# The last chunk's second product as seven half-size products, with its outputs finished one after another, and the second half starting with the chunk at the change

## The chip, the cores and the metric

The kernel runs on one core of one Trainium2 chip. The metric is the device time of one execution in microseconds (us). Engines are called as the profile calls them: PE is TensorE (matmul), PEld its weight load, DVE is VectorE, ACT is ScalarE, POOL is GpSimd, SP is SyncE, whose queue issues all DMAs here.

## The reference

```python
xn = layernorm(x)                                  # x: 2048 tokens x 576, fp32
q, k, v = phi(xn @ wq), phi(xn @ wk), xn @ wv      # 32 heads of 18
s = (phi(q) (phi(k)^T v) / (phi(q) sum phi(k))) @ wo
g = silu(gelu(xn @ w1 + b1) @ w2 + b2)             # 576 -> 4608 -> 576
out = x + s * g
```

The change lies in the last line but one and in the last: the end of the feed-forward part `g`, and the gate `x + s * g`.

## The kernel before

Each fp32 operand is split into a rounded part and a rest ("hi" and "lo"), and each product is hi·hi + hi·lo + lo·hi: a product of two operands is three matmuls. ACT makes the hi part (`set_hi`, a cast), then DVE the lo part (`set_lo`, a subtraction of two SBUF operands).

After the attention part (to about 279 us) comes the feed-forward part. The 2048 tokens are taken in two halves of 1024, and the 4608 hidden columns in `NC = 9` chunks of four blocks of 128, so there are 18 chunk steps; `step` counts them, and `base = 28 * step` is the place of a step in the plan. One step is:

- two "up" products (`Up`, pairs `n = 2 * step` and `2 * step + 1`), each a 2x2 block product done by seven half-size products (Strassen-Winograd) in the order `UP`; each of the seven is 7 matmuls of 512 columns. Between them DVE adds partial sums in PSUM and ACT applies the gelu: this gives eight tiles `g` of 128x512 (two token halves b, two column parities, two pairs `pr`);
- a "down" product with w2, again seven half-size products (`product`, `ORDER`). Product i has left operand `h[i, pr]` (made from the `g` tiles: sums `HOps.S` on POOL for i = 7, 5, 6, 3, then a cast on ACT, then a split on DVE) and right operand `W2.ops[i]`. Each product is done in two parts, `q2 = 0` and `q2 = 2`, for two of four blocks of 128 tokens each: 12 matmuls of 288 columns into one PSUM tile, which DVE then adds into `macc` in SBUF (line 1357).

DVE, ACT, POOL and PE run their instructions strictly in the order in which the code issues them (`in_order`); functions are issued at numbered places (`add(base + at, ...)`, `at_step`), and the tables `PH`, `X_AT`, `W2_NEXT` give these numbers. The SP queue is ordered by a scheduler.

In the first half of the steps the operands of w1 and w2 are made from the raw weights and stored to DRAM (`keep_op`); the second half loads them back, chunk 0 first (`n % NP`, `n % NC`).

The last step (`plain`) does not use the seven products for its down product. It loads the raw w2 of chunk 8, splits it (in step 16) and runs a plain product (`down_plain`, line 1467): eight blocks of 128 tokens one after another, 24 matmuls each. For each block DVE adds the sum to `macc` (line 1462), ACT applies the silu (line 1463), DVE multiplies by s (1420) and adds x (1421; for block 6 POOL does), and a DMA writes the rows (1422). The last block is split into 384 and 192 columns. The eight `h` operands (names `hp`) are casts and splits of `g` without sums. Before it POOL adds the shared term U1 to three parts of `macc` (`combine`, line 1367).

Of the kernel before, what the change touches and what calls it, by code (L numbers as in the profile page):

```python
# [15 lines left out]
P = 128  # L16
# [22 lines left out]
NWARM = 20  # L39

# [4 lines left out]
def linear_attention_gated_ffn(ctx, tc, x, xT, wqkv, wo, w1, w1e, b1, w2, b2, out):  # L45
# [78 lines left out]
    w1_dram, w2_dram = {}, {}  # L124

# [512 lines left out]
    def load_w2_raw(n):  # L638
        raw = w2rp.tile([P, 4, CF // 2, HD], F32, tag="w2raw", name=f"w2raw{n}")
        nc.sync.dma_start(raw.rearrange("p b a d -> p (b a d)"), w2[n % NC])  # L640
        return raw
# [207 lines left out]
    def load_we(n):  # L849

        we_sb[n] = w1p.tile([P, WB, P], F32R, tag="we", name=f"we_{n}", bufs=2)
        dst = we_sb[n].bitcast(F32).rearrange("p b c -> p (b c)")
        g, q = divmod(n % NP, WG)
# [8 lines left out]
    class W1:  # L862


        def __init__(self, n):
            self.n = n
            raw = stage_w1(f"w1raw{n}")
            nc.sync.dma_start(raw, w1[n % NP])
# [43 lines left out]
    class W1Loaded(W1):  # L912


        def __init__(self, n):
            self.n, self.tiles = n, {}
            for i in ("a", "c", "d"):
                if i == "c":
                    t = w1r.tile([P, 8, P], F32R, tag="stw", name=f"wc_{n}")
                else:  # L920
                    t = w1_tile(i, n)
                self.tiles[i] = t
                nc.sync.dma_start(t.bitcast(F32), w1_dram[n % NP, i])

    def load_six(n):

        t = w1_tile("e", n)
        for k in range(2):
            six[n + k] = t[:, 4 * k : 4 * k + 4]
            nc.sync.dma_start(six[n + k].bitcast(F32), w1_dram[(n + k) % NP, 6])  # L930
# [240 lines left out]
    class Up:  # L1171
        late = []

        def __init__(self, n, w, xs):
            self.p, self.w = n % NP, w
# [36 lines left out]
        def step(self, i):  # L1212
# [12 lines left out]
            elif i == 6:  # L1225
                self.mm(A, 6, first=False)
                nc.scalar.copy(u1_sb, A)  # L1227
                if self.p:
                    self.gelu(0, 0, B)
            elif i == 5:  # L1230
                self.mm(E, 5)
                nc.scalar.copy(m5_sb, E)
                if not self.p:
                    self.gelu(0, 0, B)
# [15 lines left out]
    class W2:  # L1250
# [21 lines left out]
        def plain(self, f):  # L1272
            k = 2 - 2 * (f % 2)
            self.src["p", f] = self.raw[:, k : k + 2, f // 2]

        def hi(self, i):
            tag = ORDER[i[1]] if isinstance(i, tuple) else i
            self.tiles[i], self.ops[i] = op_tile(fr, [2, HD], f"w2_{tag}", 1, f"w2_{self.n}_")
# [7 lines left out]
        def load(self, i):  # L1286
            t, self.ops[i] = op_tile(fr, [2, HD], f"w2_{i}", 1, f"w2_{self.n}_")
            nc.sync.dma_start(t.bitcast(F32), w2_dram[self.n % NC, i])

    class HOps:  # L1290
# [28 lines left out]
        def hi(self, i, pr):  # L1319
            self.ops[i, pr] = hi_lo(gp, [P, 512], f"h{HBUF[i, pr]}", 1, f"h{i}{pr}_")  # L1320
# [12 lines left out]
    }  # L1333
    ORDER = (1, 2, 7, 4, 5, 3, 6)
    CHAIN = {2: 1, 3: 5, 4: 7}
# [36 lines left out]
    tails = {}  # L1372

    def load_xs(t):
        F = lambda v: v.bitcast(F32)
        flat = lambda v: F(v).rearrange("p a b -> p (a b)")[:, :D]
        if t == 0:
            xt, s_t = flat(w1_tile("a", "x0")), stage_w1("s0")[:, :D]
        elif t == 1:
            xt = flat(w1_tile("a", "x1"))  # L1380
            s_t = flat(w1p.tile([P, WB, P], F32R, tag="we", name="s1", bufs=2))
        elif t == 2:
            xt, s_t = (flat(w1_tile("a", f"{v}2")) for v in "xs")
        elif t == 3:
            xt, s_t = stage_w1("x3")[:, :D], flat(w1_tile("a", "s3"))
        elif t == 4:
            raw = F(fr.tile([P, 2, D], F32R, tag="w2_5", name="xs4", bufs=1))
            xt, s_t = raw[:, 0], raw[:, 1]
        else:
            if t == 5:  # L1390
                tails["h"] = F(x_hi(2, "xs56")).rearrange("p a b -> p (a b)")
                tails["l"] = F(x_lo(2, "xs7")).rearrange("p a b -> p (a b)")
            v = {5: tails["h"], 6: tails["h"][:, 2 * D :], 7: tails["l"]}[t]
            xt, s_t = v[:, :D], v[:, D : 2 * D]
        nc.sync.dma_start(xt, x[t * P : (t + 1) * P, :])
        nc.sync.dma_start(s_t, s_dram[t])
        tails["xs", t] = xt, s_t

    def tail_split(b, f):
        src = h.A[f // 2, b, f % 2]  # L1400
        if b == 0:
            pair = hi_lo(gp, [P, 512], f"h{f}", 1, f"hp{f}_")
        else:
            k = f % 2
            if f < 2 and ("t", 0) not in tails:
                tails["t", 0] = x_lo(0, "hp0")
            if f >= 2 and ("t", 1) not in tails:
                tails["t", 1] = x_lo(1, "hp1")
            t = tails["t", f // 2]
            pair = t[:, 2 * k, :], t[:, 2 * k + 1, :]  # L1410
        set_hi(pair, src)
        tails["hs", b, f] = pair, src

    def tail_lo(b, f):
        pair, src = tails["hs", b, f]
        set_lo(pair, src, nc.vector)

    def gate(t, c, xt, s_t, cs=slice(0, D), eng=nc.vector):

        nc.vector.tensor_tensor(s_t[:, cs], c[:, cs], s_t[:, cs], op=MUL)  # L1420
        eng.tensor_tensor(s_t[:, cs], s_t[:, cs], xt[:, cs], op=ADD)
        nc.sync.dma_start(out[t * P : (t + 1) * P, cs], s_t[:, cs])


# [26 lines left out]
    def down_plain(t, ws):  # L1451

        bi, q = divmod(t, QH)
        cs = slice(q * P, (q + 1) * P)
        seq = []
        for f, (wh, wl) in enumerate(ws):
            hh, hl = tails["hs", bi, f][0]
            seq += [(hh, wh), (hh, wl), (hl, wh)]
        dst = c_tile(bi, q).rearrange("p n d -> p (n d)")

        def end(ps, c):
            nc.vector.tensor_tensor(c, ps, c, op=ADD)
            nc.scalar.activation(c, c, AF.Silu)

        def mm(ps, w, i):
            st, w_all = seq[i]
            nc.tensor.matmul(  # L1467
                ps, st[:, cs], w_all.rearrange("p n d -> p (n d)")[:, w],
                start=(i == 0), stop=(i == len(seq) - 1),
            )  # L1470

        if t < 7:
            ps = bank2(f"pd{t}")
            for i in range(len(seq)):
                for h in range(2):
                    mm(ps[:, h, :HD], slice(h * HD, (h + 1) * HD), i)
            end(ps[:, :, :HD], as2(dst))
            gate(t, dst, *tails["xs", t], eng=nc.gpsimd if t == 6 else nc.vector)
            return

        parts = [slice(0, 384), slice(384, D)]
        ps = []
        for k, w in enumerate(parts):
            n = w.stop - w.start
            ps.append(bank1(f"pd{t}_{k}")[:, :n])
            for i in range(len(seq)):
                mm(ps[k], w, i)
        for k, w in enumerate(parts):
            end(ps[k], dst[:, w])
        for w in parts:  # L1490
            gate(t, dst, *tails["xs", t], cs=w)
# [60 lines left out]
    )  # L1552
    plans = {}
# [20 lines left out]
    for step in range(n_chunks):  # L1574
# [3 lines left out]
        h = HOps(c)  # L1578
# [21 lines left out]
        elif not plain:  # L1600
# [3 lines left out]
            if step + 2 < n_chunks:  # L1604
                make(W2, w2t, step + 1)
                for i, at in W2_NEXT.items():
                    add(base + at + 10 * change, lambda i=i, n=step + 1: w2t[n].load(i))
            else:
                make(W2, w2t, step + 1)

                w = w2t[step + 1]
                add(base + 7, w.load_raw)
                for f in range(CF):
                    add(base + 22 + f, lambda f=f, w=w: (w.plain(f), w.hi(("p", f))))
                    add(base + 24 + f, w.lo, ("p", f))
        if not plain:
# [8 lines left out]
            for what in ("S", "hi", "lo"):  # L1625
                for (i, pr), at in PH[what].items():
                    add(base + at, getattr(h, what), i, pr)
# [14 lines left out]
        if plain:  # L1642
            for m in (C12, C21, C22):
                add(base + 4, combine, m, nc.gpsimd)
            for t, at in enumerate((6, 7, 12, 13, 5, 12, 12, 12)):
                add(base + at, load_xs, t)
            for b, f, at, lo in (
                (0, 0, 7, 8), (0, 1, 8, 9), (1, 0, 10, 10), (1, 1, 10, 11), (0, 2, 11, 12),
                (0, 3, 12, 13), (1, 3, 13, 13), (1, 2, 13, 13),
            ):  # L1650
                add(base + at, tail_split, b, f)
                add(base + lo, tail_lo, b, f)
# [7 lines left out]
        if plain:  # L1660
            break
# [7 lines left out]
    ws = [w2t[step].ops["p", f] for f in range(CF)]  # L1669
    for t in range(2 * QH):  # L1670
        down_plain(t, ws)
# [47 lines left out]
```

## Time and profile before

| what | value |
|---|---|
| median of 3 runs | 1092.71 us (1092.48 to 1092.85) |
| profiled execution, its own time | 1092.45 us |
| span of its trace | 1090.6 us |
| busy: PE, DVE, ACT, POOL | 1082.6, 798.2, 549.2, 454.6 us |
| one down product of a step (168 matmuls) | 22.39 us |
| last down product (192 matmuls) | 25.71 us, from 1060.17 us |
| last matmul to end of span | 4.7 us |

The profiled execution's time lies 1.85 us above its span. In the rows of the trace the first number is the start in us from the span's beginning, the second the duration; "xN" merges N instructions; the bracket gives the idle time of the engine ahead of it and what ended that.

### The profile page before, as it was taken

The page shows a single profiled execution, that of the slowest core. Times are in us where ns is not written, and L with a number is a line of the kernel's source. Part 1 is how long each engine was busy: PE and PEld are TensorE (multiplying, and loading weights), DVE is VectorE, ACT ScalarE, POOL GpSimd, SP SyncE. Part 2 cuts the span into 40 slices and gives each one's busy share as a digit, 9 for nine tenths or more (in the row PEclk, how much of TensorE's full clock was granted, in tenths as well). Part 3 has the DMA queues.
Part 4 walks back from the last instruction along what each step waited for, and adds up shares of the span by engine and source line. Part 5 has one row for each costly group of instructions (what it writes and reads, how often), then busy time and mean ns, then how long its engine had stood idle before and what let it go on. Part 6 is the DMA issues. An engine that isn't in the chain of part 4 may idle for free.

```text
span 1090.6 us, 18119 instructions
## 1 busy us (share of the span) xinstructions
PE 1082.6 (99%) x6704; PEld 1007.4 (92%) x6704; DVE 798.2 (73%) x1099; ACT 549.2 (50%) x956; POOL 454.6 (42%) x391
## 2 busy tenths in 40 slices
PE   9999999999999999999999999999999999999998
PEld 8999999999898998988989989899898998988988
DVE  7776559888688898888988988657475574664856
ACT  6545476455646456465564654624335244252552
POOL 3555414332547455464555553414325143341340
PEclk9999999999999999999999999999999999999999
DMA  7999635675958659576595669968676666767452
GB/s 239 239 222 214 212 105 192 213 246 183 343 222 316 219 192 334 170 294 237 204 330 181 258 235 408 379 233 308 224 232 214 211 228 223 231 219 222 132 184 87
DMA packets 87266, 254.58 MB, mean 233 GB/s; under 512 B 11783, under 2 KB 24071, under 8 KB 84490
## 3 DMA queue, kind: packets, MB, share of 16 engines
q1 hardware_dynamic: 87178, 253.42, 69.7%
q8 instruction: 53, 0.87, 0.3%
q14 instruction: 35, 0.29, 0.1%
HBM read 156.57 MB, written 94.58 MB: 230 GB/s over the span
## 4 chain that ended last, share of the span: by engine, by line
PE 98%; DVE 1%; SPq 0%; ACT 0%; DMA 0%; issue 0%; POOL 0%; POOLq 0%
PE pm L1351 35%; PE a L1189 16%; PE bc L1189 10%; PE e L1189 10%; PE pk L317 6%; PE ps_s L813 5%; PE pq L317 5%; PE pv L317 4%; PE pd L1467 2%; PE ps_kva L378 1%; PE ptp L795 1%; PE warm L365 0%; PE ps_kw L728 0%; PE ps_kvb L378 0%; DMA wa_rest0q<-xh 0%; SPq L963 0%
## 5 line engine op out<-in xcount | busy, mean ns | idle before, releaser
L1357 DVE TENSOR_TENSOR macc<-pm,macc 128x576 f32<-128x576 f32 x218 | 164.4, 754 | 55.5 <-PE pm L1351 54.9
L837 ACT CAST h_h<-g 128x512 fp32r<-128x512 f32 x204 | 122.6, 620 | 132.2 <-PE pm L1351 131.6
L840 DVE TENSOR_TENSOR h_l<-g,h_h 128x512 fp32r<-128x512 f32 x204 | 154.6, 769 | 14.9 <-ACT h_h L837 13.9
L1317 POOL TENSOR_TENSOR mid<-g 128x512 f32<-128x512 f32 x34 | 44.0, 1293 | 134.9 <-ACT g L1205 134.9
L1218 ACT COPY mid<-a 128x512 f32<-128x512 f32 x36 | 21.1, 587 | 110.3 <-PE a L1189 110.1
L1224 DVE TENSOR_TENSOR bc<-bc,mid 128x512 f32<-128x512 f32 x36 | 25.1, 698 | 51.5 <-PE bc L1189 40.7
L1311 POOL TENSOR_TENSOR g<-g 128x512 f32<-128x512 f32 x34 | 52.2, 1535 | 20.8 <-ACT h_h L837 16.7
L883 POOL TENSOR_TENSOR w1raw<-w1raw 128x256 f32<-128x256 f32 x18 | 13.3, 737 | 113.9 <-ACT h_h L837 65.3
L1237 DVE TENSOR_TENSOR z<-a,mid 128x512 f32<-128x512 f32 x36 | 25.1, 698 | 46.6 <-PE a L1189 46.6
L1439 POOL TENSOR_TENSOR fin1l<-fin1h,fin1l 128x288 f32<-128x288 f32 x8 | 6.5, 808 | 122.8 <-DMA fin1l<-s_dram 57.9
L1314 POOL TENSOR_TENSOR g<-g 128x512 f32<-128x512 f32 x34 | 52.6, 1546 | 7.6 <-DVE h_l L840 5.5
L1308 POOL TENSOR_TENSOR g<-g 128x512 f32<-128x512 f32 x34 | 50.3, 1481 | 2.7
L778 POOL TENSOR_TENSOR pbuf<-phiq,den 128x576 f32<-128x576 f32 x16 | 19.0, 1188 | 61.2 <-DVE den L777 57.8
L1227 ACT COPY mid<-a 128x512 f32<-128x512 f32 x36 | 21.2, 588 | 44.3 <-PE a L1189 44.3
L1238 ACT COPY mid<-a 128x512 f32<-128x512 f32 x36 | 21.1, 587 | 40.0 <-DVE z L1237 40.0
L840 DVE TENSOR_TENSOR h_l<-mid,h_h 128x512 fp32r<-128x512 f32 x34 | 38.0, 1118 | 2.4 <-ACT h_h L837 2.4
L317 PE MATMUL pk<-wkv_h,xh 128*128 128x288 f32 (+1 forms) x160 | 38.2, 321 | 0.5 <-DVE xh L245 0.5
L317 PE MATMUL pk<-wkv_l,xh 128*128 128x288 f32 (+1 forms) x160 | 38.3, 322 | 0.1
L317 PE MATMUL pq<-wq_h,xh 128*128 128x288 f32 x160 | 34.7, 298 | 0.7 <-DVE phiq L336 0.7
L813 PE MATMUL ps_s<-kw_h,th 128*128 128x288 f32 x160 | 35.2, 302 | 0.0
L765 POOL TENSOR_TENSOR eq<-phiq,zb 128x576 f32<-128x576 f32 x16 | 22.9, 1432 | 27.6 <-DMA zb<-z_dram 19.4
L317 PE MATMUL pq<-wq_l,xh 128*128 128x288 f32 x160 | 34.3, 296 | 0.0
(891 smaller groups left out, 3709.0 us busy)
## 6 DMA issues: line engine op xcount, KB each, us to landing
we<-we_dram SPq DMA_DIRECT2D x36, 448.0 KB, 5.7
w2raw<-w SPq DMA_DIRECT2D x10, 1152.0 KB
w1raw<-w SPq DMA_DIRECT2D x18, 512.0 KB, 4.8
op_a<-wa SPq DMA_DIRECT2D x18, 512.0 KB, 4.6
op_c<-wc SPq DMA_DIRECT2D x18, 512.0 KB, 4.2
op_d<-wd SPq DMA_DIRECT2D x18, 512.0 KB, 2.7
wc<-op_c SPq DMA_DIRECT2D x18, 512.0 KB, 4.6
wa<-op_a SPq DMA_DIRECT2D x18, 512.0 KB, 5.0
```

The source lines that it names most:

```text
L317: nc.tensor.matmul(ps[:, h, : ws.stop - ws.start], st, w[:, k, ws], start=(begin and i == 0), stop=(end and i == len(seq) - 1), skip_group ...
L813: nc.tensor.matmul(ps[:, h, :HD], st[:, k, :], w[:, k, h * HD : (h + 1) * HD], start=(i == 0), stop=(i == len(seq) - 1),)
L837: nc.scalar.copy(pair[0], src)
L840: eng.tensor_tensor(pair[1], src, pair[0].bitcast(F32), op=SUB)
L1189: nc.tensor.matmul(ps, st, mv, start=first and n == 0, stop=n == len(seq) - 1, skip_group_check=True,)
L1224: tt(B, B, m1_sb, op=ADD)
L1308: tt(src[5, pr], A(1, 0), A(1, 1), op=ADD)
L1311: tt(src[6, pr], src[5, pr], A(0, 0), op=SUB)
L1314: tt(src[3, pr], A(0, 1), src[6, pr], op=SUB)
L1317: tt(src[7, pr], A(0, 0), A(1, 0), op=SUB)
L1351: nc.tensor.matmul(ps[:, q, :HD], hs[p][st][:, cs], m[:, p, :], start=(n == 0 and i not in CHAIN), stop=(n == 5), skip_group_check=True,)
L1357: nc.vector.tensor_tensor(dst, src, dst, op=ADD)
```

## The change

Four things are changed.

1. The last step's down product is done by seven products too (`last_chunk`), in the order `LAST = (1, 2, 5, 3, 6, 7, 4)`, with the operands' places in `HLAST` and their issue places in a table `PL`. 168 matmuls of 288 columns take the place of 192. POOL's sums, 14 casts and 14 splits take the place of 8 casts and 8 splits.
2. Sums are kept in PSUM: products 1, 6, 7 and 4 add up in the tiles `a0` (q2 = 0) and `a1[0]`, `a1[1]` (q2 = 2), products 2, 5 and 3 use `e[0]` and `e[1]`. After each part the sum is read by DVE (`drain`); after products 2, 6, 7 and 4 one of the four output parts is final, and `gate` applies the silu (ACT), the product with s and the sum with x. For product 2 both are on POOL; for 6, 7 and the first part of 4 the product is on DVE and the sum on POOL; for the last part both on DVE.
3. The second half of the steps takes the chunks in the order 8, 0, 1, ..., 7, so the first step behind the change of halves uses chunk 8's w2 operands from SBUF, where the step before left them, and the raw load of w2 in step 16 with its four casts and splits is gone.
4. s and x are loaded in four pairs of DMAs for two blocks each (`load_gated`), and `combine` is issued at places 1 to 3 of the last step instead of 4, ahead of the two `finish` steps on POOL.

```diff
+AGAIN = (NC - 1, *range(NC - 1))
+    def chunk_of(step):
+        return step if step < NC else AGAIN[step - NC]
+    def pair_of(n):
+        return 2 * chunk_of(n // 2) + n % 2
...
-                nc.sync.dma_start(t.bitcast(F32), w1_dram[n % NP, i])
+                nc.sync.dma_start(t.bitcast(F32), w1_dram[pair_of(n), i])
...
+    HLAST = {
+        (1, 0): 0, (1, 1): 1, (2, 0): 2, (2, 1): 3, (6, 0): 4, (4, 1): 0, (5, 0): "w", (3, 0): "w",
...
+    LAST = (1, 2, 5, 3, 6, 7, 4)
...
+        def gate(b, n, q2, c, q=slice(0, 2), eng=(nc.vector, nc.gpsimd), last=False):
+            cs = slice(n * HD, (n + 1) * HD)
+            xt, st = (v[:, q, cs] for v in gated[2 * b + q2 // 2])
             nc.scalar.activation(c, c, AF.Silu)
+            to = c if last else st
+            eng[0].tensor_tensor(to, c, st, op=MUL)
+            eng[1].tensor_tensor(st, to, xt, op=ADD)
...
+        def drain(i, q2):
...
+            ps = e[q2 // 2] if e else None
+            if i == 1:
+                for a, c, _ in banks(C11):
+                    tt(c, a, c, op=ADD)
+            elif i in (2, 5, 3):
+                c = macc[:, q2 : q2 + 2, {2: C11, 5: C22, 3: C12}[i], :]
+                tt(c, ps, c, op=ADD)
+                if i == 2:
+                    gate(0, 0, q2, c, eng=(nc.gpsimd, nc.gpsimd))
+            elif i in (6, 7):
+                for a, c, to in banks({6: C12, 7: C22}[i]):
+                    tt(to, a, c, op=ADD)
+                gate(int(i == 7), 1, q2, ps)
+            else:
+                for q, (a, c, _) in enumerate(banks(C21)):
+                    tt(a, a, c, op=ADD)
+                    if q2:
+                        gate(1, 0, q2, a, q=q, eng=(nc.vector, nc.vector), last=True)
+                    else:
+                        gate(1, 0, q2, a)
+        for k, i in enumerate(LAST):
...
+                drain(i, q2)
+                at_step(base + 14 + 2 * k + q2 // 2)
...
+    PL = dict(
+        S={(7, 0): 7, (5, 0): 8, (6, 0): 9, (3, 0): 10, (7, 1): 13, (5, 1): 14, (6, 1): 15, (3, 1): 16},
...
+            if change:
+                w2t[step + 1] = w2t[step]
...
-                add(base + 7, w.load_raw)
-                for f in range(CF):
-                    add(base + 22 + f, lambda f=f, w=w: (w.plain(f), w.hi(("p", f))))
-                    add(base + 24 + f, w.lo, ("p", f))
```

Three places of the program show what stands where. In the names, `a0`, `a10`, `a11`, `e0`, `e1` are PSUM tiles, `macc` and `gated` lie in SBUF, `h_x0`, `h_x1`, `h_x3` and `wa_h` are buffers that hold left operands, `g` are gelu tiles.

The first place is POOL at the end of the last step. Before, the last sums are the `finish` steps, three `combine` and one gate:

```order
L1440 TENSOR_TENSOR fin1l_11260<-fin1l_11260,fin2h_11261 128x288
L1439 TENSOR_TENSOR fin3l_11266<-fin3h_11265,fin3l_11266 128x288
L1440 TENSOR_TENSOR fin3l_11266<-fin3l_11266,fin4h_11267 128x288
L1367 TENSOR_TENSOR macc_3316<-macc_3316 128x4x288 x3
L1421 TENSOR_TENSOR xs56_11427<-xs56_11427 128x576
```

In the changed kernel the sums for pair 1 (7, 5, 6, 3 in that order) stand there, and the two gate instructions of product 2 stand between the third and the fourth of them:

```order
L1319 TENSOR_TENSOR mid_3319<-g_11360,g_11422 128x512
L1310 TENSOR_TENSOR g_11422<-g_11422,g_11394 128x512
L1313 TENSOR_TENSOR g_11360<-g_11422,g_11360 128x512
L1440 TENSOR_TENSOR gated0_11366<-macc_3316,gated0_11366 128x2x288
L1441 TENSOR_TENSOR gated0_11366<-gated0_11366 128x2x288
L1316 TENSOR_TENSOR g_11408<-g_11408,g_11360 128x512
L1440 TENSOR_TENSOR gated1_11382<-macc_3316,gated1_11382 128x2x288
L1441 TENSOR_TENSOR gated1_11382<-gated1_11382 128x2x288
```

So the sum for operand (3, 1), the row that writes `g_11408`, has moved behind a gate that waits for product 2, its sum and its silu.

The second place is DVE in the last down product. Before, each block is a sum out of PSUM, a multiply and an add (blocks 4 and 5 here):

```order
L1462 TENSOR_TENSOR macc_3316<-pd4_11579,macc_3316 128x576
L1420 TENSOR_TENSOR xs4_11327<-macc_3316,xs4_11327 128x576
L1421 TENSOR_TENSOR xs4_11327<-xs4_11327 128x576
L1462 TENSOR_TENSOR macc_3316<-pd5_11609,macc_3316 128x576
L1420 TENSOR_TENSOR xs56_11427<-macc_3316,xs56_11427 128x576
```

In the changed kernel, from the sum of product 6 on:

```order
L1468 TENSOR_TENSOR e0_11467<-a0_11431,macc_3316 128x2x288
L1440 TENSOR_TENSOR gated0_11366<-e0_11467,gated0_11366 128x2x288
L847 TENSOR_TENSOR h41_l_11589<-g_11394,h41_h_11588 128x512
L1468 TENSOR_TENSOR e1_11468<-a10_11432,macc_3316 128x288
L1468 TENSOR_TENSOR e1_11468<-a11_11433,macc_3316 128x288
L1440 TENSOR_TENSOR gated1_11382<-e1_11468,gated1_11382 128x2x288
L1468 TENSOR_TENSOR e0_11467<-a0_11431,macc_3316 128x2x288
L1440 TENSOR_TENSOR gated2_11428<-e0_11467,gated2_11428 128x2x288
```

What moved: sum and multiply of one part still follow each other, with the silu on ACT between them, but a part is now 12 matmuls of PE instead of 24.

The third place is the SP queue in the last step of the first half, with what each row waits for (DMAHW are DMA completions). Before:

```order
L834 DMA op_c<-wc_7194 128x1024 [waits DMAHW5_49,DVE_49]
L834 DMA op_d<-wd_7213 128x1024 [waits DMAHW6_49,DVE_49]
L923 DMA wc_7409<-op_c 128x1024 [waits DMAHW7_49,Pool_49]
L834 DMA op_a<-wa_7230 128x1024 [waits DMAHW0_49,DVE_49]
L834 DMA op_6_7278<-w_17_7264 128x512 [waits DMAHW1_49,DVE_49]
```

In the changed kernel:

```order
L841 DMA op_c<-wc_7194 128x1024 [waits DMAHW5_49,DVE_49]
L841 DMA op_d<-wd_7213 128x1024 [waits DMAHW6_49,DVE_49]
L930 DMA wc_7409<-op_c 128x1024 [waits DMAHW7_49,DMAHW5_49,Pool_49]
L841 DMA op_a<-wa_7230 128x1024 [waits DMAHW0_49,DVE_49]
L841 DMA op_6_7278<-w_17_7264 128x512 [waits DMAHW1_49,DVE_49]
```

The order is the same; the load of `wc` now reads what the store two rows above writes, and waits for it too.

More of the change, by code (lines that the diff above doesn't have):

```diff
@@ L1370, in c_tile @@
         return macc[:, q, 2 * bi : 2 * bi + 2, :]
[L1372 to L1422, printed above, removed]
     def silu_first(s):
@@ L1448, in finish_tiles @@
         return tiles
[L1451 to L1491, printed above, removed]
@@ L1577, in linear_attention_gated_ffn @@
         plain = step == n_chunks - 1
-        h = HOps(c)
+        h = HOps(step)
         if half == 0:
@@ L1603, in linear_attention_gated_ffn @@
             add(base + (16 if change else 14), make, W1Loaded, w1t, 2 * step + 3)
[L1604 removed]
+            if change:
+                w2t[step + 1] = w2t[step]
+            else:
                 make(W2, w2t, step + 1)
                 for i, at in W2_NEXT.items():
[L1607 to L1611, printed above, removed]
[L1612 to L1615 removed]
+                    add(base + at, lambda i=i, n=step + 1: w2t[n].load(i))
         if not plain:
@@ L1624, in linear_attention_gated_ffn @@
                     add(base + 26 + k, combine, C21, nc.gpsimd, slice(2 * k, 2 * k + 2))
-            for what in ("S", "hi", "lo"):
-                for (i, pr), at in PH[what].items():
-                    add(base + at, getattr(h, what), i, pr)
+        for what in ("S", "hi", "lo"):
+            for (i, pr), at in (PL if plain else PH)[what].items():
+                add(base + at, getattr(h, what), i, pr)
         if half == 1 and c == 0:
@@ L1642, in linear_attention_gated_ffn @@
         if plain:
[L1643 to L1652, printed above, removed]
+            for k, m in enumerate((C12, C21, C22)):
+                add(base + 1 + k, combine, m, nc.gpsimd)
+            for k, at in enumerate((9, 10, 13, 14)):
+                add(base + at, load_gated, k)
         for j in range(CF // 2):
@@ L1660, in linear_attention_gated_ffn @@
         if plain:
+            last_chunk(h.ops, w2t[step].ops, base)
             break
```

90 lines of the change are left out of this document (73 added, 17 removed).

## The prediction

> **What bounds the kernel now.** I read the page first, then the chain of waits in order of time, PE's waits, and last the last 55 us engine by engine.
>
> ```profile
> PE 1082.6 (99%) x6704; PEld 1007.4 (92%) x6704; DVE 798.2 (73%) x1099; ACT 549.2 (50%) x956; POOL 454.6 (42%) x391
> PE 98%; DVE 1%; SPq 0%; ACT 0%; DMA 0%; issue 0%; POOL 0%; POOLq 0%
> ```
>
> PE is the bound nearly everywhere. PE's waits, whole list:
>
> ```profile
> PE warm L365 <- POOL ident masks.py:199: 2.0, 1, 2.0
> PE pq L317 <- DVE phiq L336: 0.7, 1, 0.7
> PE pk L317 <- DVE xh L245: 0.5, 1, 0.5
> ```
>
> None lies in the feed-forward part, so every operand there comes in time, and what shortens PE's work shortens the kernel as long as that stays so. The chain's pieces for the change of halves and the last two down products:
>
> ```profile
> 658.35 22.39 PE pm L1351 x168
> ...
> 1015.53 22.39 PE pm L1351 x168
> 1060.17 25.71 PE pd L1467 x192
> ```
>
> PE ends at 1060.17 + 25.71 = 1085.88; the span is 1090.6. In the last product DVE works hard, but keeps up. One block there, DVE then ACT:
>
> ```profile
> 1076.23 0.76 DVE L1462 TENSOR_TENSOR macc<-pd,macc 128x576 f32<-128x576 f32 x1 [0.18 <-PE pd L1467]
> 1077.74 0.76 DVE L1420 TENSOR_TENSOR xs<-macc,xs 128x576 f32<-128x576 f32 x1 [0.75 <-ACT macc L1463]
> 1078.53 0.76 DVE L1421 TENSOR_TENSOR xs<-xs 128x576 f32<-128x576 f32 x1
> 1077.02 0.69 ACT L1463 ACTIVATE macc<-macc 128x576 f32<-128x576 f32 x1 [2.56 <-DVE macc L1462]
> ```
>
> Sum, silu, multiply and add follow each other with 0.03 between them; DVE stands 0.75 waiting for the silu. Sum to end of add is 1079.29 - 1076.23 = 3.06, and PE's block takes 25.71 / 8 = 3.21. The margin is 0.15 per block. This is the stage that decides.
>
> **The change part by part.** *PE's work.* 168 matmuls as in every other down product: 22.39 in place of 25.71, -3.32, all on the path. A part (one product for two blocks, 12 matmuls) is 22.39 / 14 = 1.60.
>
> *Serial work on DVE from product 6 on.* The widths needed, from the end of before:
>
> ```profile
> 1084.69 0.55 DVE L1462 TENSOR_TENSOR macc<-pd,macc 128x384 f32<-128x384 f32 x1
> 1085.90 0.36 DVE L1462 TENSOR_TENSOR macc<-pd,macc 128x192 f32<-128x192 f32 x1 [0.66 <-PE pd L1467]
> 1085.27 0.53 ACT L1463 ACTIVATE macc<-macc 128x384 f32<-128x384 f32 x1 [1.29 <-DVE macc L1462]
> 1086.30 0.36 ACT L1463 ACTIVATE macc<-macc 128x192 f32<-128x192 f32 x1 [0.49 <-DVE macc L1462]
> 1087.63 0.36 DVE L1421 TENSOR_TENSOR xs<-xs 128x192 f32<-128x192 f32 x1
> ```
>
> 288 columns lie halfway: 0.455 on DVE, about 0.46 on ACT. An independent DVE instruction starts 0.08 before the end of the one ahead (1020.35 + 0.76 against 1021.02, below). So a q2 = 0 part costs DVE 0.76 + 0.03 + 0.70 (silu) + 0.03 + 0.76 - 0.08 = 2.20; a q2 = 2 part, with two sums of 0.455, 2.27. PE makes one every 1.60: by the order, DVE stands during each silu with the next sum behind it. From the sum of (6, q2 = 0) to the end: 2.20 + 0.61 (the split of (4,1), between) + 2.27 + 2.20 + 2.27 + 2.20 for five parts = 11.75; the last part is two chains of sum, silu, multiply, add of 288 columns, 4 x 0.455 + 3 x 0.03 = 1.91, the second starting 1.83 behind the first: 3.74. Together 15.5. PE needs only 5 x 1.60 = 8.0 more from there; it waits for DVE, since product 7 adds into the bank that DVE has yet to read.
>
> *Waits before product 6.* Whether a DVE split and a POOL instruction run side by side (DVE, then POOL, step 16):
>
> ```profile
> 1014.91 0.69 DVE L840 TENSOR_TENSOR h_l<-g,h_h 128x512 fp32r<-128x512 f32 x1
> ...
> 1018.75 0.76 DVE L1357 TENSOR_TENSOR macc<-pm,macc 128x576 f32<-128x576 f32 x1 [0.84 <-PE pm L1351]
> 1019.42 0.86 DVE L840 TENSOR_TENSOR h_l<-mid,h_h 128x512 fp32r<-128x512 f32 x1
> 1020.35 0.76 DVE L1357 TENSOR_TENSOR macc<-pm,macc 128x576 f32<-128x576 f32 x1
> 1021.02 0.96 DVE L840 TENSOR_TENSOR h_l<-g,h_h 128x512 fp32r<-128x512 f32 x1
> 1017.07 1.30 POOL L1317 TENSOR_TENSOR mid<-g 128x512 f32<-128x512 f32 x1 [3.37 <-ACT g L1205]
> 1018.44 1.29 POOL L1308 TENSOR_TENSOR g<-g 128x512 f32<-128x512 f32 x1
> 1019.81 1.62 POOL L1311 TENSOR_TENSOR g<-g 128x512 f32<-128x512 f32 x1
> 1021.51 1.63 POOL L1314 TENSOR_TENSOR g<-g 128x512 f32<-128x512 f32 x1
> ```
>
> They don't. The split from 1019.42 ends at 1020.28, 0.55 after POOL's sum ends at 1019.73; the one from 1021.02 at 1021.98, again 0.55 after POOL's end at 1021.43. POOL's next sums take 1.62 in place of 1.29. A sum out of PSUM (1018.75) stays at 0.76. [...]
>
> ACT at the head of the last product, POOL's price for 576 columns, and a weight load starting 0.13 ahead of its matmul:
>
> ```profile
> 1061.04 0.69 ACT L1205 ACTIVATE g<-bc,b1c 128x512 f32<-128x512 f32 x1
> 1061.62 1.13 ACT L837 CAST hp<-g 128x512 fp32r<-128x512 f32 x2
> 1062.77 1.28 ACT L1463 ACT_TABLE_LOAD   x1
> 1084.90 1.41 POOL L1421 TENSOR_TENSOR xs<-xs 128x576 f32<-128x576 f32 x1 [31.38 <-DVE xs L1420]
> 1082.18 0.49 PEld L1467 LDWEIGHTS pd<-w__11159,hp 128*128 128x128 f32 x3
> 1082.31 0.68 PE L1467 MATMUL pd<-w__11159,hp 128*128 128x384 f32 x3
> ```
>
> Now the walk, in us after 1060.17; a cast is 0.62, a split 0.69. POOL's sums (7,1), (5,1), (6,1) follow the gelu's end at 1.56 and end by 5.97. The table load ends by 3.4, unhurt.
> - Product 2's first part ends at 4.80: sum 4.83 to 5.59, silu to 6.31, and only behind it the cast of (5,1), 6.21 to 6.83. PE wants it at 6.80: wait 0.19. Its split is ready to run at 6.86, but POOL multiplies 6.34 to 7.75, so it ends at 8.30. PE wants it at 7.26: wait 1.20.
> - Product 3 adds into the banks of product 5, whose sum on DVE stands behind the split of (7,0). That follows its cast (10.22, behind the second silu) and POOL's sum (3,1), 9.66 to 10.95, so it ends at 11.50, and the sum 11.42 to 12.18. PE wants the bank at 10.99: wait 1.35.
> - (3,1): POOL's sum ends at 10.95 since the gate (multiply to 7.75, add to 9.58) stands ahead of it; cast to 11.60; split from 12.10, held by POOL's second multiply, to 13.33. PE wants it at 13.01: wait 0.48 with the weight load.
>
> Together 3.22. The sum of (6, q2 = 0) then starts at 9 x 1.60 + 3.22 + 0.05 = 17.66.
>
> *The tail.* Before, the last DVE end is 1087.99 and the span's end 2.61 later, for a transfer of 192 columns; with 288 I keep 2.61 (nothing to 0.3 more).
>
> *The order of chunks, loads, `combine`.* At the change of halves:
>
> ```profile
> 636.48 0.32 SPq L834 DMA_DIRECT2D op_c<-wc  x1
> 637.75 0.32 SPq L834 DMA_DIRECT2D op_d<-wd  x1
> 638.16 0.41 SPq L923 DMA_DIRECT2D wc<-op_c  x1
> op_c<-wc SPq DMA_DIRECT2D x18, 512.0 KB, 4.2
> ```
>
> The load of 638.16 must now wait until the store lands at 636.48 + 4.2 = 640.7, and stores queued behind it on SP move by up to 2.5. The operand is used after 658.35 + 22.39 = 680.74: cost 0, and at most those 2.5 if the 40 us of cover were gone. Seven loads and one raw load fall away where PE waits for none: 0. `combine` goes ahead of `finish` on POOL, whose first sum for this step needs a gelu at about 1052: 0. Four casts and splits fewer in step 16: 0.
>
> *Sum.* 14.39 + 3.27 + 15.5 + 2.61 = 35.8 after 1060.17: a span of 1095.9, +5.3 on 1090.6. The profiled execution took 1092.45 (span plus 1.85), which gives 1097.8; the median of the runs is 0.26 above it: 1098.0. A measurement of this kernel can tell about 0.2%, or 2.2 us, from no change.
>
> **The rivals.** *POOL and DVE don't hinder each other here.* Same walk with splits of 0.69 and undelayed sums: the waits are 0.19, 0.45, 0.79 and 0.44, so 1.87 in place of 3.22: 1096.7. For it: POOL's gate reads other buffers than any row above. Against it: the rows. Chance 0.15.
>
> *Only the serial chain counts.* POOL and ACT come early enough, and nothing waits before product 6: 14.4 + 15.5 + 2.6 = 32.5, span 1092.7, +2.1, so 1094.8. Chance 0.06: it needs a POOL gate at a fraction of 1.41.
>
> *Faster: PE stays the bound.* If DVE could take the next sum during a silu, a part would cost it 0.76 + 0.76, under 1.60. PE would end at 1060.17 + 22.39 = 1082.56. The first of the last two chains starts 0.80 before that and ends 1.91 later, the second 1.83 after the first begins plus 1.91: 1085.5; plus 2.61, 1088.1, -2.5: 1090.2. It decides from the point where a part costs DVE no more than 1.60, against 2.20 by the rows and the order. Chance 0.05.
>
> *Slower still.* With PE waiting about 4.8 in 27 us the granted clock may drop:
>
> ```profile
> 1085.90:1090.60 4.70, 0.00 (x0) 0.00 (x0) 2.02 (x5) 0.36 (x1) 0.42 (x1) 0.73 0.33 126
> ```
>
> In the 4.7 us without a matmul the mean clock (0.73, third from the end) falls. At half clock a part takes 3.2 and is the bound again: six parts at +1.0 over DVE's 2.2, about 1104. No wait in the walk is over 1.4, so chance 0.05.
>
> **How the numbers follow.** The forecast holds 0.69. Its own spread comes from the unknown prices: no delay between engines gives 1097.5, 0.06 in place of 0.03 gives 1098.7, silu in PSUM at 0.78 1098.4, POOL at 1.20 for 1.41 gives 1097.4. The range of 8 in 10 goes from 1095.4 (between the chain alone and the first rival) to 1100.5 (a first touch of the clock). Faster by over 0.2%: 0.05. Within 0.2%: 0.07 (most of the second rival and some of the first). Slower: 0.88.
>
> **What the profile will show.** Right: PE waits of 4 to 5 us in the last product, put down to DVE splits and sums at products 5, 3, 7 and 4; DVE 0.7 idle before each multiply, with ACT as releaser; the chain's last 15 us on DVE and ACT; splits over 1 us beside POOL's gate; no PE wait near 680. Wrong: splits at 0.69 beside POOL, DVE idle before its sums of products 6 and 7 (then PE is ahead), or new waits in earlier steps.

## The result, and the profile after

| | before | after |
|---|---|---|
| median | 1092.7 us (1092.48 to 1092.85) | 1098.4 us (1098.21 to 1098.59) |
| ratio to before | | 1.0052, 95% interval 1.0035 to 1.007 |
| profiled execution: own time, span | 1092.45, 1090.6 us | 1098.21, 1096.5 us |

The change costs 5.7 us; the forecast was 1098.0, 5.3 above before. Two later executions at a lower granted clock, one of the kernel before (1526.0 us, clock 0.66) and one of e9_casts_first (1789.1 us, clock 0.56), are in no time below. Engine totals and the chain's shares from the page of the kernel after:

```profile
PE 1080.5 (99%) x6680; PEld 1003.9 (92%) x6680; DVE 801.2 (73%) x1102; ACT 549.8 (50%) x958; POOL 479.3 (44%) x407
PE 95%; DVE 2%; ACT 1%; issue 1%; SPq 0%; DMA 0%; POOL 0%; DVEq 0%; ACTq 0%; POOLq 0%
```

PE has 24 matmuls and 2 us of work less, and 3% of the chain that ended last has gone from PE to DVE, ACT and the time between them. PE's waits, whole list (line, what it waited for, us in total, times, longest):

```profile
PE warm L372 <- POOL ident masks.py:199: 2.0, 1, 2.0
PE e L1492 <- DVE h_x L847: 1.2, 2, 1.0
PE a L1492 <- DVE e L1468: 1.0, 1, 1.0
PE e L1492 <- DVE macc L1463: 1.0, 1, 1.0
PE pq L324 <- DVE phiq L343: 0.7, 1, 0.7
PE pk L324 <- DVE wkv_l L518: 0.6, 1, 0.6
PE pk L324 <- ACT xh L249: 0.5, 1, 0.5
```

The three rows with L1492 are new, and all lie in the last product. (The row with L518 lies at the head of the kernel and comes and goes between the runs.) That stage by itself (PE, PEld, DVE, ACT, POOL busy, then the granted clock):

```profile
1060.45:1087.85 27.40, 24.01 (x169) 22.24 (x167) 20.83 (x30) 10.85 (x18) 16.84 (x11) 1.00 0.37 134
```

It takes 27.40 us for 168 matmuls that take 22.39 elsewhere, at a clock of 1.00: 5.0 us of standing. The list shows 3.2 of it, since it counts a matmul as busy to its modelled end (0.30 us here), while in a row without a wait the next one starts after 0.13 (22.39 / 168); the shortest wait that it counts here is 0.23.

### The profile page after: what moved, and what is told of

The parts are those of the page before. It is cut to its first block, busy times and chain, and to the rows that moved or that the text cites. A ratio compares the mean times of both kernels' runs of the same rounds, so it can differ in the third digit from the quotient of the medians.

```text
span 1096.5 us, 18090 instructions
## 1 busy us (share of the span) xinstructions
PE 1080.5 (99%) x6680; PEld 1003.9 (92%) x6680; DVE 801.2 (73%) x1102; ACT 549.8 (50%) x958; POOL 479.3 (44%) x407
## 4 chain that ended last, share of the span: by engine, by line
PE 95%; DVE 2%; ACT 1%; issue 1%; SPq 0%; DMA 0%; POOL 0%; DVEq 0%; ACTq 0%; POOLq 0%
PE pm L1369 35%; PE a L1196 16%; PE bc L1196 10%; PE e L1196 10%; PE pk L324 6%; PE ps_s L820 5%; PE pq L324 5%; PE pv L324 4%; PE ps_kva L385 1%; PE ptp L802 1%; PE a L1492 0%; PE e L1492 0%; PE warm L372 0%; PE ps_kw L735 0%; DVE e L1468 0%
## 5 line engine op out<-in xcount | busy, mean ns | idle before, releaser
L844 ACT CAST h_h<-g 128x512 fp32r<-128x512 f32 x210 | 126.1, 620 | 134.0 <-PE pm L1369 132.7
L847 DVE TENSOR_TENSOR h_l<-g,h_h 128x512 fp32r<-128x512 f32 x210 | 160.5, 775 | 15.0 <-ACT h_h L844 13.9
L1319 POOL TENSOR_TENSOR mid<-g 128x512 f32<-128x512 f32 x36 | 46.6, 1293 | 138.8 <-ACT g L1212 138.8
L1313 POOL TENSOR_TENSOR g<-g 128x512 f32<-128x512 f32 x36 | 55.1, 1531 | 20.9 <-ACT h_h L844 16.7
L1316 POOL TENSOR_TENSOR g<-g 128x512 f32<-128x512 f32 x36 | 55.4, 1540 | 7.7 <-DVE h_l L847 5.5
L1310 POOL TENSOR_TENSOR g<-g 128x512 f32<-128x512 f32 x36 | 53.6, 1488 | 2.8
```

Of the source, the lines that this page charges most:

```text
L844: nc.scalar.copy(pair[0], src)
L847: eng.tensor_tensor(pair[1], src, pair[0].bitcast(F32), op=SUB)
L1310: tt(src[5, pr], A(1, 0), A(1, 1), op=ADD)
L1313: tt(src[6, pr], src[5, pr], A(0, 0), op=SUB)
L1316: tt(src[3, pr], A(0, 1), src[6, pr], op=SUB)
L1319: tt(src[7, pr], A(0, 0), A(1, 0), op=SUB)
```

## The experiments

All times are medians, the lengths are those of the profiled execution; each kernel was timed beside runs of the kernel before, whose median was 1092.74 to 1092.81. The last product is followed by three lengths: from the start of DVE's first sum of the stage (1062.08 in the kernel after) to the sum of (6, q2 = 0), from there to DVE's last end, and from there to the end of the span.

| kernel | us | to sum (6, q2 = 0) | to DVE's last end | tail |
|---|---|---|---|---|
| after | 1098.4 | 16.07 | 15.54 | 2.81 |
| e2_seven_alone | 1098.4 | 16.09 | 15.54 | 3.05 |
| e8_sum_first | 1098.1 | 15.82 | 15.54 | 2.82 |
| e7_write_only | 1097.8 | 15.50 | 15.54 | 2.81 |
| e3_front | 1096.0 | 13.83 | 15.53 | 2.81 |
| e4_defer | 1096.3 | 16.09 | 12.63 | 3.26 |
| e5_front_defer | 1093.55 | 13.84 | 12.62 | 3.33 |
| e6_all | 1091.7 | 12.86 | 11.14 | 3.84 |
| e10_add_on_dve | 1092.0 | 12.87 | 12.32 | 2.84 |
| e9_casts_first | 1100.9 | 19.33 | 15.54 | 2.77 |
| e11_filled | 1099.1 | 16.71 | 15.54 | 2.85 |
| e12_filled_some | 1100.4 | 18.23 | 15.54 | 2.78 |

**The order of chunks alone, and the seven products alone.** The first (e1_order_alone) puts only the new chunk order into the kernel before, the second (e2_seven_alone) takes only that out of the kernel after.

```diff
 (kernel before)
+AGAIN = (NC - 1, *range(NC - 1))
...
+            if change:
+                w2t[step + 1] = w2t[step]
 (kernel after)
-AGAIN = (NC - 1, *range(NC - 1))
+AGAIN = tuple(range(NC))
```

> The kernel before with the new chunk order of the second half alone (chunk 7 first at the change, its tiles kept, the last step still the plain product of the last chunk in order). Theory (the order of the chunks and its loads cost nothing): the time of before, 1092.7 within 1 us, and no wait of TensorE near 680 us. Rival (the chunk at the change, or a load that reads what was stored late, costs something): 1 us or more above before, with a wait of TensorE at the change or at a chunk's first product. If the whole 5.7 us came from the order, 1098.4.

> The changed kernel with the old chunk order (the tiles of the last chunk are stored and loaded again for the last step; the second product of the last step stays in seven half-size products). Theory (all of the 5.7 us is the last product): 1098.4, within 1 us, TensorE waits again about 5 us behind the stage's start. Rival (the order carries part of the loss): lower than 1098.4 by that part, down to 1092.7.

Measured: 1092.5 (ratio 1.0, 0.9991 to 1.0009) and 1098.4 (1.0056, 1.0043 to 1.007). The order and the load that follows a store of the same data are worth nothing that can be measured; all of the 5.7 us comes with the last product. The raw load of w2 is still there in the first kernel and gone in the second, so it was not timed by itself; nor was the earlier `combine`. No wait of PE points at either. PE's waits with the order alone, whole list, show none near the change of halves:

```profile
PE warm L372 <- POOL ident masks.py:199: 2.0, 1, 2.0
PE pq L324 <- DVE phiq L343: 0.7, 1, 0.7
PE pk L324 <- ACT xh L249: 0.4, 1, 0.4
```

**What stands ahead of product 6.** POOL's sum (3,1) goes ahead of the gate, and two casts go ahead of the silus (e3_front).

```diff
 PL (S, then hi)
-        ... (6, 1): 15, (3, 1): 16},
+        ... (6, 1): 15, (3, 1): 15},
-            (5, 1): 16, (7, 0): 17, (3, 1): 18,
+            (5, 1): 15, (7, 0): 15, (3, 1): 18,
```

> The changed kernel with three instructions of the last product earlier: POOL's sum (3,1) ahead of its first gate, and the two casts of (5,1) and (7,0) on ScalarE ahead of the silus. Theory (the time goes by two chains in a row: TensorE's waits ahead of product 6, then the serial work on VectorE from product 6 to the end): the waits ahead of product 6 fall from 3.2 us to 1 or less, the last sum starts that much earlier, and the time falls by 2.7 us to about 1095.7. Rival (VectorE and POOL as such are the bound, whatever the order in which they are issued): no change, 1098.4, with the waits of TensorE moved to later products.

Measured: 1096.0 (1.0032, 1.0019 to 1.0044), 2.4 less than after. The first length falls by 2.24, the second stays to 0.01. The waits ahead of product 6 are gone; in the feed-forward part only this row is left:

```profile
...
PE a L1492 <- DVE e L1468: 1.8, 3, 1.0
...
```

The splits still take 0.97 to 1.25 us beside POOL's sum and gate (1.15 to 1.50 in the kernel after), but they come earlier, so that PE no longer waits for them. So what made the waits was when DVE's and POOL's work was issued. DVE is not idle now: from 1065.22 to the sum of (6, q2 = 0) at 1075.86 it has no gap, and the chain that ended last runs over it.

**The standing at the silu.** The multiply and add of a part on DVE are issued behind the next part's sum (e4_defer).

```diff
+            def rest():
                 to = c if last else st
                 eng[0].tensor_tensor(to, c, st, op=MUL)
                 eng[1].tensor_tensor(st, to, xt, op=ADD)
...
+            for f in held:
+                f()
+            if eng[0] is nc.vector and not last:
+                waiting.append(rest)
```

> The changed kernel with the multiply and the add of each part on VectorE issued behind the next part's sum, so that VectorE need not stand while ScalarE's silu runs; all parts but the last half part. Theory (VectorE's standing at each silu is part of the chain that sets the end, at two parts ahead of product 6 and at two behind it): 3.2 us less, about 1095.2. Rival (what VectorE waits for is covered by other work, as idle time of an engine that is not the bottleneck): 1098.4; or worse, since an add that comes later keeps a bank or a tile longer: above 1098.4.

Measured: 1096.3 (1.0033, 1.002 to 1.0045): 2.1 less instead of 3.2. The first length stays (16.09), the second falls by 2.9, since DVE now has the next sum to do. DVE there:

```profile
1082.30 0.77 DVE L1480 TENSOR_TENSOR e<-a,macc 128x576 f32<-128x576 f32 x1
1082.98 0.75 DVE L1443 TENSOR_TENSOR gated<-e,gated 128x576 f32<-128x576 f32 x1
1083.83 1.04 DVE L1480 TENSOR_TENSOR e<-a,macc 128x288 f32<-128x288 f32 x2
1084.77 0.75 DVE L1443 TENSOR_TENSOR gated<-e,gated 128x576 f32<-128x576 f32 x1
```

The idle time of 0.70 ahead of these multiplies is gone. Ahead of the split (4,1) DVE still stands 1.23 us, since the cast for it comes behind the silu on ACT. And the tail has grown from 2.81 to 3.26, and the profiled execution (1095.55) was 0.7 below the median of its runs.

**Both, and two steps more.** One kernel has both edits (e5_front_defer). Another (e6_all) also interleaves the last part's two chains of 288 columns and moves the operands of product 4.

```diff
-            if eng[0] is nc.vector and not last:
+            if eng[0] is nc.vector:
...
+                if q2:
+                    waiting.pop()()
 PL (hi, lo)
-            ... (4, 1): 22,
+            ... (4, 1): 19,
-            ... (4, 0): 21, (4, 1): 22,
+            ... (4, 1): 22, (4, 0): 23,
```

> The changed kernel with both edits: the three instructions ahead of the gate, and each part's multiply and add behind the next part's sum. Theory (two links of one chain: the early instructions shorten it ahead of product 6, the deferral takes VectorE's standing out of what is left): 5.3 us less than the changed kernel by the walk of the prediction with these instructions moved, about 1093.1; with the 2.1 that the deferral alone brought, not 3.2, about 1094. Rival (both shorten the same wait, so that the second brings nothing): 1095.9.

> The changed kernel with both edits, and two more: the last half part's two chains of 288 columns interleaved (the second sum ahead of the first multiply), and the cast (4,1) at position 19, its split at 22 and the split (4,0) at 23. Theory (with TensorE hardly waiting and the serial end shortened, the seven products' lower TensorE time of 22.4 us sets the end): the last instruction of VectorE about 2 us earlier than with both edits alone, 1091 to 1092, below the kernel before (1092.7). Rival (the serial work on VectorE behind product 6 cannot be covered by the shorter order of products): 1093 or more, no better than before.

Measured: both edits together 1093.55 (1.0008, 0.9999 to 1.0017), 4.85 less than after, against 2.4 + 2.1 = 4.5 for the sum of the two; the lengths are those of the two apart (13.84 and 12.62). These are two links of one chain. With all four edits 1091.7 (0.9991, 0.9982 to 1.0): the 11 runs (1091.52 to 1092.11) lie below each of the runs of before beside them (from 1092.42). The gain of 1.0 us is at the edge of what the interval can tell. PE's waits, whole list:

```profile
PE warm L372 <- POOL ident masks.py:199: 2.0, 1, 2.0
PE pq L324 <- DVE phiq L343: 0.7, 1, 0.7
PE pk L324 <- ACT xh L249: 0.4, 1, 0.4
```

PE now makes the last product without a listed wait, and its 22.4 us can be had. The split (4,0) no longer stands ahead of the sum of (6, q2 = 0), and the first length is 1.0 shorter than with two edits. The chain in order of time shows where PE hands over to DVE:

```profile
1063.62 9.68 PE e L1506 x72
1073.30 1.60 PE a L1506 x12
...
1074.92 0.04 DVE e L1480
```

From there DVE works with gaps of 0.1 us at most to its last end, 11.14 us later, so that DVE and not PE sets the end. Of the 3.3 us that PE's work is below the plain product, only 1.0 shows in the time: from PE's end to DVE's it is 3.2 us instead of 2.1, and the tail is 3.84 instead of 2.61.

**Where the tail comes from.** It goes from 2.81 to 3.84 between after and the kernel with all four edits. One add is moved from POOL to DVE (e10_add_on_dve).

```diff
-                        gate(1, 0, q2, a)
+                        gate(1, 0, q2, a, eng=(nc.vector, nc.vector))
```

> The kernel with all four edits (1091.7), with the add of the part (4, q2=0) on VectorE instead of POOL. Theory (behind VectorE's last instruction the end waits for the stores, which POOL's three adds in a row make late; the time from VectorE's last instruction to the end has grown from 2.8 to 3.8 us): VectorE ends 0.75 us later, but POOL's last add comes 1.4 us earlier, the time behind VectorE's last instruction goes back to about 2.8 us, and the sum is 0.3 us less, 1091.4. Rival (the longer end has nothing to do with POOL's adds and their stores): 0.75 us more, 1092.5.

Measured: 1092.0 (0.9991, 0.9982 to 1.0), between the two. POOL with all four edits, then DVE and POOL in this kernel:

```profile
1081.74 4.14 POOL L1444 TENSOR_TENSOR gated<-gated 128x576 f32<-128x576 f32 x3 [0.42 <-DVE gated L1443]
```

```profile
1084.32 1.14 DVE L1444 TENSOR_TENSOR gated<-gated 128x576 f32<-128x576 f32 x1
...
1082.06 2.79 POOL L1444 TENSOR_TENSOR gated<-gated 128x576 f32<-128x576 f32 x2 [0.42 <-DVE gated L1443]
```

With three adds in a row POOL ends at 1085.88, next to DVE's last end (1086.06), and three stores come together. With two it ends at 1084.85, 2.7 ahead of DVE's (1087.56), and the tail is 2.84: the theory holds for the tail. SP's rows show how, with all four edits and then in this kernel:

```profile
1085.91 0.37 SPq L1451 DMA_DIRECT2D out<-gated  x1
1086.33 0.96 SPq L1448 DMA_DIRECT2D out<-gated  x2
```

```profile
1084.87 0.99 SPq L1451 DMA_DIRECT2D out<-gated  x2
1086.72 1.21 SPq L1448 DMA_DIRECT2D out<-gated  x2
```

SP issues these stores one after another (1085.91 to 1086.28, then from 1086.33). The store of POOL's last add stands ahead of DVE's two (L1448), so that the first of these, ready at 1085.20, is issued only at 1086.33, and the last issue ends 1.23 us behind DVE's end; in this kernel it ends 0.37 behind. That is 0.86 of the 1.00. What DVE pays for the add was put too low: it took 1.14, not 0.75; it ran beside POOL's add and ended 0.61 behind it. -1.00 in the tail and +1.18 in DVE's length make +0.2; the medians differ by as much, which is less than either kernel's spread.

**Why the splits are long.** POOL's gate of product 2 becomes writes of a constant (e7_write_only); this kernel leaves out the multiply by s and the sum with x there.

```diff
+            if (b, n) == (0, 0):
+                for _ in range(2):
+                    nc.gpsimd.memset(c, 0.0)
+                    nc.gpsimd.memset(c, 0.0)
+                    nc.gpsimd.memset(c[:, 0], 0.0)
```

> The changed kernel with the gate of product 2 on POOL (multiply and add of 576 columns, read and write SBUF) replaced by POOL writes of a constant, of about the same length in all; the gate of product 2 is left out. Theory (a VectorE split is held by a POOL instruction that reads two SBUF operands, and not by POOL's being busy): the splits beside the writes take about 0.7 us, where they took 1.2 to 1.5, and the time falls by about 0.8 us to 1097.6. Rival (POOL's being busy is what slows VectorE, or the long splits have another cause): they stay above 1 us, 1098.4.

Measured: 1097.8 (1.0048, 1.0033 to 1.0062), 0.6 less. DVE and POOL at the first gate in the kernel after, and in this one:

```profile
1067.29 1.50 DVE L847 TENSOR_TENSOR h_x<-g,h_x 128x512 fp32r<-128x512 f32 x1 [1.26 <-ACT h_x L844]
...
1070.72 1.15 DVE L847 TENSOR_TENSOR h_x<-mid,h_x 128x512 fp32r<-128x512 f32 x1 [1.26 <-ACT h_x L844]
...
1066.83 1.41 POOL L1440 TENSOR_TENSOR gated<-macc,gated 128x576 f32<-128x576 f32 x1 [0.47 <-ACT macc L1438]
...
1070.03 1.29 POOL L1316 TENSOR_TENSOR g<-g 128x512 f32<-128x512 f32 x1
```

```profile
1067.36 0.69 DVE L847 TENSOR_TENSOR h_x<-g,h_x 128x512 fp32r<-128x512 f32 x1 [1.26 <-ACT h_x L844]
...
1069.98 0.69 DVE L847 TENSOR_TENSOR h_x<-mid,h_x 128x512 fp32r<-128x512 f32 x1 [1.26 <-ACT h_x L844]
...
1066.88 0.58 POOL L1442 MEMSET macc<- 128x576 f32 x1 [0.46 <-ACT macc L1438]
1067.52 0.58 POOL L1443 MEMSET macc<- 128x576 f32 x1
```

After: POOL ends at 1068.24, the split at 1068.79, 0.55 later; the second pair, 1071.32 and 1071.87, again 0.55. Beside writes the split takes 0.69, though POOL is as busy, writing from 1066.88 to 1070.18 with gaps of 0.06. So it was POOL's multiply and add, which read SBUF, that held the split (1.50 and 1.15), and not POOL's being busy, and keeping the gate from it is worth 0.6 us on this path. POOL's sum (3,1), which reads too, is still there.

**The sum alone, the casts alone.** The two halves of the edit that brought 2.4 (e8_sum_first, e9_casts_first).

```diff
 PL, S
-        ... (6, 1): 15, (3, 1): 16},
+        ... (6, 1): 15, (3, 1): 15},
 PL, hi, in the other kernel
-            (5, 1): 16, (7, 0): 17, (3, 1): 18,
+            (5, 1): 15, (7, 0): 15, (3, 1): 18,
```

> The changed kernel with POOL's sum (3,1) alone ahead of its first gate; the casts stay behind the silus. Theory (the two early waits of TensorE stand behind each other, so that taking one away leaves the other): 0.3 us less, about 1098.1. Rival (the sum is what was late): most of what the three moved instructions brought, about 1096.

> The changed kernel with the two casts (5,1) and (7,0) alone ahead of ScalarE's silus; POOL's sum (3,1) stays behind the first gate. Theory (the sum and the casts are late at the same time, each hides the other): 0.3 us less than the changed kernel, about 1098.1, as with the sum alone, where both together brought 2.4. Rival (the casts carry what both brought): about 1096.

Measured: the sum alone 1098.1 (1.0049, 1.0036 to 1.0062), as expected: with the casts still late it brings 0.3, no more than the spread of the runs (its first length is 0.25 shorter). The casts alone 1100.9 (1.0073, 1.006 to 1.0087): 2.5 slower than after, which neither theory had. Its runs spread from 1100.2, at a mean granted clock of 0.997, to 1102.2, at 0.994; the profiled one took 1101.2 (0.994), the number that the next expectations use. The waits ahead of product 6 gather mostly into one, and the granted clock falls (PE's longest wait, then the row of ACT that holds the cast (3,1), then PE's busy time, matmuls, clock, DMA share, GB/s in three stretches):

```profile
PE e L1492 <- ACT h_x L844: 2.7, 1, 2.7
...
1072.09 1.14 ACT L844 CAST h_x<-g 128x512 fp32r<-128x512 f32 x2 [3.67 <-POOL g L1316]
```

```profile
1070.10:1074.00 3.90, 0.56 (x2) 0.89 0.21 76
1074.00:1079.60 5.60, 5.57 (x23) 0.50 0.15 53
1079.60:1084.00 4.40, 4.40 (x34) 0.96 0.00 0
```

PE runs on to (3,1) without a pause, stands there for 2.66 us, as the cast waits for POOL's sum (3,1), which is still behind the gate, and works at half clock (0.50) in the 5.6 us of the second stretch. The table load of the silu now also stands behind the casts (it starts at 1065.86 instead of 1062.44), the first of which waited 2.59 us for POOL's sum, so that the gate starts 6.2 us behind DVE's first sum (1067.92) instead of 4.75 (1066.83), and with it everything behind it on POOL comes later.

**The clock, or the late gate?** The same kernel with work put into the pause: one matmul of product 3 repeated, 15 times and in a second kernel 4 times (e11_filled, e12_filled_some), so that its term counts 16 and 5 times.

```diff
+                        if i == 3 and q2 + q == 0 and n == 3:
+                            for _ in range(15):
+                                nc.tensor.matmul(
+                                    ps, hs[0][0][:, cs], wh[:, 0, :], start=False, stop=False,
```

> The kernel with the two casts first (1101.2), with 15 further matmuls of product 3 (the first of its matmuls repeated, so that this term counts 16 times) ahead of the matmul that waits 2.7 us for the cast (3,1): 2.0 us of work inside the pause. Theory (the loss of that kernel is TensorE's clock, which fell to half for 6.7 us after the pause of 2.66 us): no half clock, the last stretch at full speed, the sum of (6, q2=0) at 16.4 to 16.5 behind the first sum instead of 19.3, and about 1098.8. Rival (the loss comes from the silu behind the casts and the later gate on POOL, and the clock costs nothing, since VectorE is the bound): 1101.2.

> The same with 4 further matmuls instead of 15 (0.5 us, the first matmul of product 3 counts 5 times), so that a pause of about 2.1 us remains. Theory (it is the length of a pause that lets the clock fall; pauses of 1.0 us left it at 1.00, one of 2.66 us did not): if the limit lies above 2.1 us, 1098.8 as with the full filling; if below, the half clock stays and the time is about 1101. Rival as for the full filling: 1101.2 with or without a fall of the clock.

Measured: 1099.1 with 15 (1.0059, 1.0045 to 1.0073) and 1100.4 with 4 (1.007, 1.0057 to 1.0082). The clock with 15, then with 4:

```profile
1070.00:1080.00 10.00, 8.55 (x63) 1.00 0.16 59
```

```profile
1075.00:1075.50 0.50, 0.50 (x5) 0.90 0.00 0
1075.50:1078.50 3.00, 3.00 (x14) 0.50 0.27 98
1078.50:1079.00 0.50, 0.50 (x5) 0.68 0.00 0
```

More work on PE makes the kernel 1.8 us faster: of the 2.5 us, 1.8 were the clock, and the 0.7 that are left are put down to the late gate (the first length is 16.71 instead of 16.07). With a pause of 2.15 us left, the clock falls too, but later and for a shorter time, and the time is 1.3 above that with 15.

## Why the prediction was right, point by point

- **PE's work** (-3.32): 168 matmuls take 22.4 us when nothing is late, as the kernel with all four edits shows. "All on the path" was too much: even there PE is the chain only up to the sum of (6, q2 = 0). The prediction's own sum is right in this, since it counts only nine parts of PE, 14.39.
- **Waits before product 6** (3.22): the sum of (6, q2 = 0) starts at 1078.15, 17.70 behind the stage's start at 1060.45; forecast 17.66. The three ends of splits that the walk gave, 8.30, 11.50 and 13.33, came at 8.34, 11.42 and 13.25. PE's rows name what the walk named:

```profile
1068.84 0.40 PE L1492 MATMUL e<-w__11169,h_x 128*128 128x288 f32 x1 [1.00 <-DVE h_x L847]
...
1072.59 0.66 PE L1492 MATMUL e<-w__11201,wa_h 128*128 128x288 f32 x3 [0.97 <-DVE macc L1463]
...
1073.75 0.40 PE L1492 MATMUL e<-w__11201,h_x 128*128 128x288 f32 x1 [0.23 <-DVE h_x L847]
```

- **The serial chain on DVE** (15.5): 15.54, with two small misses that cancel. The silu out of PSUM took 0.64, not 0.70, and 0.40, not 0.46; but a pair of sums of 288 columns took 1.03 where two of 0.455 less the overlap were put at 0.83. One part and the next, ACT then DVE:

```profile
1078.95 0.64 ACT L1438 ACTIVATE e<-e 128x576 f32<-128x576 f32 x1 [5.42 <-DVE e L1468]
...
1078.15 0.77 DVE L1468 TENSOR_TENSOR e<-a,macc 128x576 f32<-128x576 f32 x1
1079.62 0.76 DVE L1440 TENSOR_TENSOR gated<-e,gated 128x576 f32<-128x576 f32 x1 [0.70 <-ACT e L1438]
1080.29 0.68 DVE L847 TENSOR_TENSOR h_l<-g,h_h 128x512 fp32r<-128x512 f32 x1
1080.89 1.03 DVE L1468 TENSOR_TENSOR e<-a,macc 128x288 f32<-128x288 f32 x2
```

- **The tail** (2.61): 2.81, inside the 0.3 that was left open for the wider transfer. The start of the stage moved by 0.28, which the prediction did not have; in the experiments it moves by about as much from run to run. With these the span is 0.6 above the forecast 1095.9; the profiled execution's own time lies only 1.7 above its span instead of 1.85, which gives some of it back.
- **Order, loads, `combine`** (0): for the order and the load behind a store shown by the order alone at 1092.5. For the missing raw load and for `combine` it is not shown by a run of their own; the sum leaves little for them, at most the 0.28 by which the stage starts later.
- **The rivals.** POOL and DVE not hindering each other was priced at 1096.7, 1.3 below the forecast; the run in which the gate no longer holds the splits gives 1097.8, 0.6 below after; there POOL's sum (3,1) still met a split and took 1.67 us, not 1.29. The second rival, with nothing late ahead of product 6, is what e3_front makes: 1096.0 and not 1094.8, since its splits stay long beside POOL. The faster rival's mechanism is half right: without the standing at the silu, and with the early waits gone too, PE has no listed wait, but behind product 6 DVE sets the end. It reached 1091.7, not 1090.2, since DVE ends 0.6 later than the rival had it and the tail is 1.2 longer. The clock rival was put at 0.05 because no wait exceeded 1.4 us; in this stage none did, and the clock stayed at 1.00. In e9_casts_first and e12_filled_some, where the longest wait of the stage was 2.66 and 2.15 us, it fell to 0.50.

What stays open: how much of the 0.7 us of the late gate is the table load and how much the casts, and after how much standing the clock falls.

## What to carry to other kernels

When the bound engine is given less work, add up the serial chain on the engines that empty its results: here sum, silu and multiply took 2.1 to 2.5 us per part against 1.60 of matmuls, until the next sum was issued ahead of what waits for the silu. Late pieces that hide each other have to be moved together: the pair brought 2.4 us, one alone 0.3, the other alone cost 2.5. Look at the granted clock around TensorE's pauses too: here pauses of 1.0, 0.97 and 0.23 us within 6 us left it at 1.00, and after one of 2.15 with one of 0.74 behind it it was 0.50.

## What the runs showed of the hardware that was not expected

In e12_filled_some the granted clock fell from 1.00 to 0.50 after a pause of 2.15 us followed by 0.53 us of work and one of 0.74. It fell late. With 4 matmuls in the pause PE's rows with waits are:

```profile
1073.17 0.53 PE L1498 MATMUL e<-w__11201,h_x 128*128 128x288 f32 x2 [2.15 <-ACT h_x L844]
1074.44 0.40 PE L1498 MATMUL e<-w__11201,h_x 128*128 128x288 f32 x1 [0.74 <-DVE h_x L847]
```

PE stopped at 1071.02 and worked without a pause from 1074.44; the clock fell at 1075.4, in the middle of work. Of the 4.4 us from the stop to the fall PE had worked 0.53 + 0.97 = 1.50. The clock stayed at 0.50 for 3.4 us there, and for 6.8 us (1073.1 to 1079.9) behind the pause of 2.66 us in e9_casts_first, where it fell 3.0 us after PE's stop at 1070.10, with about 0.35 us of work between. The length of a pause alone does not settle it: behind the last matmul, with PE idle to the end, the clock fell after 2.1 us in the kernel before (1085.9 to 1088.0) and after 3.1 us in the kernel after (1087.9 to 1091.0).

With all four edits the stores that SP issued behind that of POOL's last add set the end, although POOL is 44% busy in the kernel after: the 1.0 us by which the tail grew (2.81 to 3.84) went away when one of three adds left POOL (2.84).
